# Regrouping the first two score chunks, and moving the second head pair's loads and preparation forward, in an attention and feed-forward kernel

## The chip, the cores and the metric

The kernel runs on one core of a Trainium2 chip. The metric is the device time of one execution in microseconds (us). The times of single runs are also given as the span of the trace, from first to last instruction; it is some 1.8 us shorter than the time (416.1 against 417.99 in the profiled run of the kernel before). PE does the matmuls and transposes, ACT the exponentials, DVE conversions, copies and sums; POOL issues most loads. The granted clock is the share of PE's full clock that the record of the trace gives, 1.00 or 0.50 ("half clock").

## The reference

64 heads (8 batches of 8), 1152 keys, 576 pooled queries (means of two neighbours), head size 64; then two dense layers multiplied with each other and two more layers.

```python
q_pool = q.reshape(B, H, S // 2, 2, D).mean(axis=3)
scores = (1.0 / np.sqrt(D)) * np.matmul(q_pool, k.transpose(0, 1, 3, 2))
attn = softmax(scores)
x = (attn @ v) -> (B*576, H*D)
out = ((x @ w1) * (x @ w2)) @ w3 @ w_out
```

## The kernel before

Heads go in pairs. The scores of all pairs are one long row of columns, 5184 (9 key blocks of 576 queries) for each pair, cut into 324 chunks of 512. A chunk is a few matmuls into a PSUM tile (one half for each head of the pair) and one exponential of 128 x 1024 elements on ACT. Iterations hold three chunks each; between them PE does value matmuls (`pv`), transposes of the next pair (`prep_groups`), of w3 (`w3_group`) and the feed-forward layers.

```python
js = (slice(0, 2), slice(2, 5), slice(5, NJ))   # pair 0: key blocks, three groups
...
        spin(25, 128)        # dummy matmuls, to keep PE's clock up
        stage_keys(0); move_keys(0)
        spin(8, 128)
        queries(0)           # first half of pair 0's queries: 256 of 576
        spin(6, 128)
        queries(1)           # the other 320
        spin(1)
        stage_keys(1)        # DVE: second key group to fp16
...
    def scores(c):
        t = psum.tile([128, 2, CH], FP32, tag="psc", bufs=3, name="psc")
        if 3 <= c < 10:      # filler matmul for the clock
            nc.tensor.matmul(t[:, 0], ones[:, 0:128], ones, start=True, stop=True)
        ...                  # columns c*512 to c*512+511, block by block
...
    load_v(0)                # load queue, in this order
    load_w3(0, 1)
    load_q(1)
    load_k(1)                # "pair 1's keys" below
    load_w3(1, 1)
    load_wo(0)
...
    early = [(1, w3_group(0)), (3, w3_group(1))]      # (iteration, group)
...
        if prepped < NPE:    # at the end of iteration 2: pair 1, after chunk 8
            if it >= first_it(prepped) - (1 if prepped < 5 else 2):
                queue[0:0] = prep_groups(prepped)
```

Chunks 0 to 9 belong to pair 0, and pair 1 begins inside chunk 10. PE runs in program order, so whatever stands in front of chunk 9 on PE must be done before it.

The softmax here doesn't subtract the row's maximum and nothing guards it: scores larger than these inputs give would overflow.

## Time and profile before

| | before |
|---|---|
| time, three runs | 416.72, 416.95, 418.05 us |
| span of the profiled run | 416.1 us |
| PE busy / ACT busy | 406.8 / 326.3 us |
| exponential 0 / 4 / 9 starts | 7.81 / 11.86 / 16.97 us |
| granted PE clock, 7.74 to 11.15 us | 0.50 |

The prediction shows the page and the chain of waits.

### The profile page before, as it was taken

The page shows a single profiled execution, that of the slowest core. Times are in us where ns is not written, and L with a number is a line of the kernel's source. Part 1 is how long each engine was busy: PE and PEld are TensorE (multiplying, and loading weights), DVE is VectorE, ACT ScalarE, POOL GpSimd, SP SyncE. Part 2 cuts the span into 40 slices and gives each one's busy share as a digit, 9 for nine tenths or more (in the row PEclk, how much of TensorE's full clock was granted, in tenths as well). Part 3 has the DMA queues.
Part 4 walks back from the last instruction along what each step waited for, and adds up shares of the span by engine and source line. Part 5 has one row for each costly group of instructions (what it writes and reads, how often), then busy time and mean ns, then how long its engine had stood idle before and what let it go on. Part 6 is the DMA issues. An engine that isn't in the chain of part 4 may idle for free.

```text
span 416.1 us, 12696 instructions
## 1 busy us (share of the span) xinstructions
PE 406.8 (98%) x5489; PEld 270.3 (65%) x5489; DVE 197.9 (48%) x407; ACT 326.3 (78%) x356; POOL 121.1 (29%) x161
## 2 busy tenths in 40 slices
PE   7999999999999999999999999999999999999996
PEld 5577787766676577666865686667765876544443
DVE  2455755464545553555455634544455434713141
ACT  4999989989888888988888899898888889133332
POOL 6543331243435163334433414343430000000000
PEclk8999999999999999999999999999999999999999
DMA  8999999699999999999799959999994250050402
GB/s 188 203 205 187 187 206 193 117 138 161 159 180 204 174 174 183 216 140 176 137 212 150 172 86 197 157 150 152 185 171 93 44 89 20 14 117 2 101 0 103
DMA packets 96249, 59.76 MB, mean 144 GB/s; under 512 B 65472, under 2 KB 86464, under 8 KB 96192
## 3 DMA queue, kind: packets, MB, share of 16 engines
q0 software_dynamic: 26928, 32.97, 50.8%
q1 hardware_dynamic: 69264, 25.97, 36.0%
q8 instruction: 43, 0.70, 0.7%
q14 instruction: 14, 0.11, 0.1%
HBM read 67.11 MB, written 9.44 MB: 184 GB/s over the span
## 4 chain that ended last, share of the span: by engine, by line
PE 91%; ACT 5%; DMA 1%; issue 1%; SPq 0%; DVE 0%; ACTq 0%
PE po L340 20%; PE psc L315 19%; PE pa L434 16%; PE pp L457 16%; PE pb L434 15%; ACT er L325 5%; PE pT L418 3%; DMA er<-in_k_dram 1%; PE w3t L406 1%; PE psc L305 1%; PE t L169 0%; PE tk L169 0%; SPq L192 0%; DVE kc L210 0%; SPq L189 0%
## 5 line engine op out<-in xcount | busy, mean ns | idle before, releaser
L325 ACT ACTIVATE er<-psc 128x1024 f16<-128x1024 f32 x324 | 307.5, 1027 | 41.3 <-PE psc L315 41.0
L340 PEld LDWEIGHTS <-er 128*128 128x128 f16 x2880 | 103.4, 97 | 22.0 <-issue 5.9
L340 PE MATMUL po<-vt,er 128*128 128x65 f16 x2880 | 110.4, 193 | 0.0
L315 PE MATMUL psc<-qT,kT 64*128 64x512 f16 (+7 forms) x1152 | 95.1, 286 | 3.0 <-ACT er L325 2.5
L451 DVE TENSOR_TENSOR gT<-pb,asb 128x512 f16<-128x512 f32 x72 | 50.1, 695 | 55.8 <-PE pb L434 55.1
L434 PE MATMUL pa<-xT,w1sb 128*128 128x512 f16 x288 | 74.2, 380 | 0.0
L434 PE MATMUL pb<-xT,w2sb 128*128 128x512 f16 x288 | 74.1, 380 | 0.0
L457 PE MATMUL pp<-T,gT 128*128 128x256 f16 (+1 forms) x488 | 67.9, 292 | 0.0
L315 PEld LDWEIGHTS <-kT 64*128 64x128 f16 x1152 | 45.4, 94 | 28.1 <-issue 9.5
L457 PEld LDWEIGHTS <-gT 128*128 128x128 f16 x488 | 45.6, 98 | 18.5 <-issue 3.7
L444 DVE COPY asb<-pa 128x512 f32<-128x512 f32 x56 | 38.7, 691 | 39.3 <-PE pa L434 38.1
L434 PEld LDWEIGHTS <-w2sb 128*128 128x128 f16 x288 | 26.4, 98 | 32.7 <-issue 3.9
L434 PEld LDWEIGHTS <-w1sb 128*128 128x128 f16 x288 | 25.0, 98 | 30.1 <-issue 6.2
L121 POOL TENSOR_TENSOR qp<-qst 128x1152 f16<-128x1152 f16 x12 | 28.3, 2355 | 53.5 <-issue 26.5
L469 DVE TENSOR_SCALAR osb<-pp 128x256 f32<-128x256 f32 x49 | 20.8, 424 | 39.2 <-PE pp L457 39.2
L353 DVE RECIPROCAL rz<-po 128x5 f32<-128x5 f32 x64 | 12.4, 194 | 48.5 <-PE po L340 48.1
L141 POOL COPY kc<-kst 128x576 int32<-128x576 int32 x24 | 16.4, 683 | 55.8 <-issue 43.7
L357 DVE TENSOR_TENSOR xn<-po,rz 128x320 f16<-128x320 f32 x64 | 31.5, 492 | 2.2
L95 POOL DMA_DIRECT2D vst<-in_v_dram x32 | 23.4, 741 | 11.8 <-DVE T L422 5.0
L466 ACT ACTIVATE osb<-pp 128x512 f32<-128x512 f32 (+1 forms) x12 | 7.0, 579 | 24.0 <-PE pp L457 21.8
L88 POOL DMA_DIRECT2D kst<-in_k_dram x31 | 22.6, 742 | 9.2 <-DVE kT L285 2.6
L81 POOL DMA_DIRECT2D qst<-in_q_dram x31 | 19.2, 621 | 11.4 <-DMA vst<-in_v_dram 3.5
(49 smaller groups left out, 140.6 us busy)
## 6 DMA issues: line engine op xcount, KB each, us to landing
vst<-in_v_dram POOLq DMA_DIRECT2D x32, 288.0 KB, 10.3
qst<-in_q_dram POOLq DMA_DIRECT2D x31, 288.0 KB, 7.0
kst<-in_k_dram POOLq DMA_DIRECT2D x31, 288.0 KB, 12.4
out_dram<-osb SPq DMA_DIRECT2D x66, 128.0 KB, 2.6
w3h<-in_moe_w_dram POOLq DMA_DIRECT2D x3, 512.0 KB, 14.7
xT<-in_moe_w_out_dram POOLq DMA_DIRECT2D x4, 256.0 KB, 10.7
w1sb<-in_moe_w_dram POOLq DMA_DIRECT2D x2, 512.0 KB, 16.3
w2sb<-in_moe_w_dram POOLq DMA_DIRECT2D x2, 512.0 KB, 17.0
```

What stands on the lines that cost most here:

```text
L88: nc.gpsimd.dma_start(out=kst[P].rearrange("p u j d -> p u (j d)"), in_=k[b, h0:h0 + 2].rearrange("u (p j) d -> p u (j d)", j=NJ))
L95: nc.gpsimd.dma_start(out=vst[P].rearrange("p u j d -> p u (j d)"), in_=v[b, h0:h0 + 2].rearrange("u (p j) d -> p u (j d)", j=NJ))
L121: eng.tensor_tensor(out=qps[pp][r].rearrange("p c u d -> p u c d"), in0=src[:, :, :, 0, :], in1=src[:, :, :, 1, :], op=ALU.add)
L315: nc.tensor.matmul(t[:, u, o:o + ln].rearrange("p (c f) -> p c f", f=64), kT[P][s, j, :], qT[P][s, f0 // 64:(f0 + ln) // 64], start=True, ...
L325: nc.scalar.activation(out=er[:, :, r:r + CH], in_=psc.pop(c), func=AF.Exp, bias=0.0, scale=SCALE)
L340: nc.tensor.matmul(po[P, u][:, VW * x:VW * x + D + 1], er[:, u, r:r + 128], vts[P % 4][:, u, j, 0:D + 1], start=(m == 0), stop=(m == 44), ...
L357: nc.vector.tensor_tensor(out=xn[:, P % 2, :, u, :], in0=acc[:, :, 0:D], in1=rz.to_broadcast([128, 5, D]), op=ALU.mult)
L434: nc.tensor.matmul(p, w[:, mc, ft * 128:ft * 128 + 128], xT[:, mc, t0:t0 + 512], start=(mc == 0), stop=(mc == NC - 1))
L444: nc.vector.tensor_copy(out=asb[ft], in_=p)
L451: nc.vector.tensor_mul(out=o, in0=p, in1=a)
L457: nc.tensor.matmul(p[:, 0:n], gT[:, ft, 128 * i:128 * i + 128], T16[:, ft, n * s:n * s + n], start=(ft == 0), stop=(ft == NF - 1))
L469: nc.vector.tensor_scalar_mul(out=osb, in0=p[:, 0:n], scalar1=1.0 / (SCL * SCL))
```

## The change

The intent is to start ACT earlier and to have pair 1 ready earlier. Chunk 0 is made of the first 256 queries of key blocks 0 and 1, so that it needs only the first query half; chunk 1 takes the rest of both. Pair 1's loads go ahead of w3, pair 1 is prepared ahead of chunk 8, the w3 transposes go to later iterations and one filler is deleted.

```diff
-        js = (slice(0, 2), slice(2, 5), slice(5, NJ))
+        js = (slice(0, 2), slice(2, 4), slice(4, NJ))
...
-        spin(6, 128)
+        spin(5, 128)
+        scores(0)
+        expo(0)
         queries(1)
...
-        if 3 <= c < 10:
+        if 3 <= c < 9:
...
+        if c < 2:
+            pieces = [[(0, 0, 256), (1, 0, 256)], [(0, 256, 320), (1, 256, 192)]][c]
...   (expo: chunk 0 written with a strided output, chunk 1 as two ACTIVATEs)
     load_v(0)
-    load_w3(0, 1)
     load_q(1)
     load_k(1)
+    load_w3(0, 1)
     load_w3(1, 1)
...
-    early = [(1, w3_group(0)), (3, w3_group(1))]
+    early = [(3, w3_group(0)), (4, w3_group(1))]
...
+            if it == 2 and w == 2:
+                queue[0:0] = prep_groups(1)
+                prepped = 2
+                group("F")
+                group("X")
+            if it or w:
-            scores(BURST * it + w)
-            expo(BURST * it + w)
+                scores(BURST * it + w)
+                expo(BURST * it + w)
```

More of the change, by code (lines that the diff above doesn't have):

```diff
@@ L303, in scores @@
         psc[c] = t
-        if 3 <= c < 10:
+        if 3 <= c < 9:
             nc.tensor.matmul(t[:, 0], ones[:, 0:128], ones, start=True, stop=True)
+        pieces = []
         g = c * CH
         while g < (c + 1) * CH:
-            J = g // SQ
+            J, f0 = divmod(g, SQ)
+            pieces.append((J, f0, min(SQ - f0, (c + 1) * CH - g)))
+            g += pieces[-1][2]
+        if c < 2:
+            pieces = [[(0, 0, 256), (1, 0, 256)], [(0, 256, 320), (1, 256, 192)]][c]
+        o = 0
+        for J, f0, ln in pieces:
             P, j = divmod(J, NJ)
-            f0 = g - J * SQ
-            ln = min(SQ - f0, (c + 1) * CH - g)
-            o = g - c * CH
             for u in range(2):
-                s = slice(64 * u, 64 * u + 64)
-                nc.tensor.matmul(t[:, u, o:o + ln].rearrange("p (c f) -> p c f", f=64), kT[P][s, j, :],
-                                 qT[P][s, f0 // 64:(f0 + ln) // 64], start=True, stop=True)
-            g += ln
+                x = slice(64 * u, 64 * u + 64)
+                nc.tensor.matmul(t[:, u, o:o + ln].rearrange("p (c f) -> p c f", f=64), kT[P][x, j, :],
+                                 qT[P][x, f0 // 64:(f0 + ln) // 64], start=True, stop=True)
+            o += ln
     def expo(c):
@@ L324, in expo @@
             assert nb >= 90 * Pg + 45 + 5 * Jg + 5
-        nc.scalar.activation(out=er[:, :, r:r + CH], in_=psc.pop(c), func=AF.Exp,
-                             bias=0.0, scale=SCALE)
+        t = psc.pop(c)
+        if c == 0:
+            io = [(er[:, :, 0:2 * SQ].rearrange("p u (j f) -> p u j f", j=2)[:, :, :, 0:256],
+                   t.rearrange("p u (j f) -> p u j f", j=2))]
+        elif c == 1:
+            io = [(er[:, :, 256:SQ], t[:, :, 0:320]), (er[:, :, SQ + 256:2 * CH], t[:, :, 320:CH])]
+        else:
+            io = [(er[:, :, r:r + CH], t)]
+        for o, i in io:
+            nc.scalar.activation(out=o, in_=i, func=AF.Exp, bias=0.0, scale=SCALE)
     po, xns = {}, {}
```

## The prediction

> **What bounds the kernel now.** I read the page first (shares, slices, chain), then the chain of waits for the first 45 us, then the timeline of the first 18 us, because every edit of this change lies there.
>
> ```profile
> PE 406.8 (98%) x5489; PEld 270.3 (65%) x5489; DVE 197.9 (48%) x407; ACT 326.3 (78%) x356; POOL 121.1 (29%) x161
> ...
> PE   7999999999999999999999999999999999999996
> ...
> PE 91%; ACT 5%; DMA 1%; issue 1%; SPq 0%; DVE 0%; ACTq 0%
> ```
>
> PE is busy for 406.8 of 416.1 us, and 91% of the chain that ended last is PE. So over the whole kernel PE work is the bound, and all of PE's idle time is 9.3 us. By stretches, the idle time is 2.2 us in 0 to 10, none in 10 to 15, 0.7 in 15 to 20, 1.1 in 20 to 40, 1.7 in 40 to 80, and 3.5 after 300. A reordering at the start can recover only part of the early idle time, plus whatever PE instructions it deletes.
>
> The chain of the start, in order of time (start, length, what):
>
> ```profile
> 2.23 5.12 DMA er<-in_k_dram
> 7.36 0.02 issue
> 7.38 0.76 DVE kc L210
> 8.15 0.05 issue
> 8.19 0.50 PE tk L169 x3
> 8.69 0.43 PE spin L198
> 9.12 0.54 PE psc L315 x3
> 9.66 0.54 PE psc L305
> 10.20 0.54 PE psc L315 x4
> 10.74 0.54 PE tk L169 x4
> ...
> 12.47 0.55 PE w3t L406 x8
> ...
> 16.97 1.93 ACT er L325 x2
> ```
>
> The reader should see that the first exponential is not on it. The path is the second key load of pair 0 (lands at 7.35), its conversion, its transposes, and then PE without a break from 8.19 to 16.95, up to the scores of chunk 9. ACT bounds the next stretch, from 16.97 to 23.5.
>
> The timeline shows the onset and the one gap:
>
> ```profile
> 5.94 0.37 ACT L245 CAST qT<-tq 128x256 f16<-128x256 f32 x1 [1.69 <-PE tq L242]
> 6.52 0.34 PE L240 MATMUL tq<-ident,er 64*64 64x64 f16 x10 [0.17 <-DVE er L231]
> 6.91 0.33 DVE L245 COPY qT<-tq 128x320 f16<-128x320 f16 x1 [0.44 <-PE tq L240]
> 7.81 8.93 ACT L325 ACTIVATE er<-psc 128x1024 f16<-128x1024 f32 x9 [1.49 <-PE psc L315]
> 16.97 22.32 ACT L325 ACTIVATE er<-psc 128x1024 f16<-128x1024 f32 x24 [0.24 <-PE psc L315]
> ```
>
> The first query half is in SBUF at 6.31, but exponential 0 starts at 7.81, because chunk 0 also needs the second half (ready 7.24). Nine exponentials follow, then 0.24 us of idle ACT before chunk 9. From narrow windows of the timeline they start at 7.81, 8.73, 9.70, 10.78, 11.86, 12.79, 13.88, 14.80 and 15.70. Chunks 2, 3 and 4 start 0.04 us after PE finishes their scores (9.66, 10.74, 11.82), so those three are limited by PE, not by ACT.
>
> **What the Trainium skill says.** "ScalarE: Activation LUTs", section "What ACT_TABLE_LOAD costs": an ACTIVATE with immediate scale and bias takes 186 ns + 0.833 ns per element, and back-to-back ones overlap by about 93 ns. For 1024 elements that is 1039 ns and a pitch of 946; the trace agrees, with 1027 ns and a pitch of 930 (22.32 us for 24). So splitting one exponential costs about 93 ns (an estimate from that page).
>
> "TensorE: Matmul & The Clock Gate", Part 1: a matmul starts at half clock, one per N/1.2 ns, and a free-running window of about 3.4 us of activity releases it. The trace agrees: 25 spins of 128 columns take 2.82 us, and a score chunk costs 0.54 us of chain until 10.74 and 0.32 from 11.5. The same page, Part 3, "The mechanism": matmuls start and end in program order. So a group that waits holds all PE work behind it; that is what both moved groups risk.
>
> "DMA: Bandwidth & Descriptors", "Two DMAs through the same engine are not ordered": descriptors of one queue start in order. The trace agrees in effect: loads issued in the order v0, w3 row block 0, q1, k1, w3 row block 1 release POOL's next issues at 11.21, 12.16, 13.51, 14.88 and 16.10.
>
> **Part 1, the first two chunks.** Chunk 0 becomes columns 0 to 255 of key blocks 0 and 1, which need only the first query half.
> - Release: the last such wait took 7.38 - 7.24 = 0.14 us, so its scores start at 6.31 + 0.14 = 6.45. They stream 512 columns per head as before (two pairs of 256), and exponential 0 comes 7.81 - 7.38 = 0.43 later, at 6.88: **0.93 us earlier**.
> - These scores stand ahead of the transposes of the second query half, which move from 6.52 to 6.88. Their copy ended 7.24 - 6.52 = 0.72 after they began: now 7.60, so 0.36 later.
> - Chunk 1 starts at 7.60 + 0.14 = 7.74 and is ready at 8.17. The order listing shows its second ACTIVATE with no wait, so the first waits for all four matmuls. ACT idles for some 0.3 us from 7.85 and is free again near 8.17 + 0.93 + 0.09 = 9.2.
>
> **Part 2, key groups of 2 and 5 blocks instead of 3 and 4.** Conversion of the first group starts at 7.62 (behind the later query copy), not 7.38, but is two thirds as long: 0.50, ending 8.12 against 8.13. Its transposes follow chunk 1 on PE: 8.17 + 0.33 = 8.50. The copy out takes 0.28 instead of 0.36 and ends near 8.83 against 9.09. Chunk 2 is ready at 8.86 + 0.54 = 9.40 against 9.66, chunk 3 at 10.48 against 10.74: **0.26 earlier**.
>
> Chunk 4 then pays. It needs key blocks 3 and 4. Before, block 4 was in the earlier group, and chunk 4 did not wait for the later group's copy. Now block 4 comes with the later group: five transposes, 0.54 x 5/4 = 0.67, to 11.15; copy out 0.04 + 0.42 x 5/4 = 0.57, to 11.72; a pair of 256 columns at full clock, half of 0.32, to 11.88. Exponential 4 starts at 11.92 against 11.86. **So I expect the gain of the first chunk to be spent here**, and PE to stand still for some 0.2 us that it did not stand before.
>
> **Part 3, pair 1 ahead of w3 and ahead of chunk 8.** From 11.88, PE has chunk 5 (0.64 with its filler matmul), 9 value matmuls (0.27), chunks 6 and 7 (1.28), preparation of pair 1 (0.26 + 0.61 = 0.87) and chunk 8 (0.64): 3.70, to 15.58. The w3 transposes (0.55) are gone from this stretch. Exponentials at the old pitch from 4 to 8, (15.70 - 11.86)/4 = 0.96, reach chunk 8 at 15.76: just covered. Then 13 value matmuls (0.40) and chunk 9 (0.34, its filler of about 0.3 deleted) are ready at 16.32, before ACT needs them at 16.72. The gap of 0.24 closes: exponential 9 at 16.72 against 16.97.
>
> Do the loads allow it? k1 moves from fourth to third: 11.21 + 1.35 + 1.37 = 13.93 by the spacings above. Its conversion (0.46) ends at 14.39. PE reaches the key transposes at about 14.07 + 0.35 = 14.42. Slack: almost none.
>
> **Later.** The w3 transposes (0.55 us) move to the group of iteration 3, and those of the second row block to iteration 4. Between 16.97 and 23.5 ACT bounds, and PE idles 0.52 us at 19.36, so most of the moved work fits there. Then PE is the bound and its total is smaller by one filler of 512 columns (0.3) and one short spin (0.1, but that is in time when PE waits anyway). The memory behind w3 lands in the same order; nothing later in the load queue moves. Sum: -0.25 at chunk 9, up to another -0.1 from the filler, some of it given back to moved work: **-0.3 us**.
>
> **Rivals.**
> 1. The whole 0.93 us of the first exponential survives: 416.0. For it: ACT bounds stretches up to 80 us. Against it: chunks 2 to 4 start when PE is done, so an earlier ACT only waits.
> 2. k1 lands later than 13.9, or the copies of pair 1 stall PE in front of chunk 8; 1 us late is nearly 1 us lost, 417.5 to 418. For it: slack near zero and in-order PE. Against it: it moves up by one load in a queue that keeps its order.
> 3. The clock: fewer spins and a stall let the half clock last one window more. 3.4 us at half clock is 1.7 us of PE work: 418.3. Against it: the new early scores fill what the spin leaves, and the stretch from 7.7 stays dense.
> 4. Nothing: chunk 4's wait gives all back and moved w3 work eats the gap: 416.95.
>
> **Range and chances.** 416.95 - 0.3 gives 416.6. The three runs before spread from 416.72 to 418.05, more than the effect. Rival 1 sets the low end with some spread, 415.7; rivals 2 and 4 with run noise the high end, 417.5. Two per cent is 8.3 us, more than all idle time before 300 us, so faster has 0.01; slower would need several rivals at once, 0.01.
>
> **What would show it.** First exponential at about 6.9 (step 1); a PE wait for the DVE copy of keys before chunk 4, exponential 4 within 0.2 of 11.86 (step 2); no ACT gap before chunk 9, which starts near 16.7 (step 3); total PE idle time smaller by under 0.5. I am wrong if exponential 4 is already 0.5 or more earlier, if a gap opens before chunk 8, or if the half clock lasts beyond 11.5.

## The result

| | before | after |
|---|---|---|
| median of the first comparison, 4 runs each | 417.17 us | 416.23 us |
| range | 416.72 to 418.05 | 416.03 to 416.70 |
| span of the profiled run | 416.1 us | 414.9 us |

The ratio of after to before is 0.9976, with a 95% interval of 0.9957 to 0.9996. Ratios here are the mean time of one kernel's runs over that of the other's runs of the same rounds, so not quite the ratio of the medians. 416.23 lies in the predicted range. Later calls ran the kernel before 39 more times (median 416.88, mean 416.99, from 416.13 to 419.28) and after 5 more times; all 9 runs of after have a median of 416.46 and a mean of 416.48, from 416.03 to 417.15. So the change is worth about 0.4 to 0.5 us, on a kernel whose own runs spread over 3 us. This pools several chips and has no interval of its own; by the ratios of runs of the same rounds it is 1.0 us in the first comparison and 0.3 us in the second (r_after below). The profiled run of after was the slowest of its four, that of before among the slowest of its kind.

The page of the kernel after, the lines that answer to the prediction's first fence:

```profile
PE 406.0 (98%) x5489; PEld 270.4 (65%) x5489; DVE 198.8 (48%) x407; ACT 326.3 (79%) x357; POOL 121.2 (29%) x161
...
PE   8999999999999999999999999999999999999996
...
PE 90%; ACT 6%; DMA 1%; issue 1%; SPq 0%; DVE 0%; ACTq 0%
```

Nothing changes in the large; PE's idle time is 8.9 us instead of 9.3, smaller by under 0.5 as predicted. The chain of waits of the kernel after, first 18 us:

```profile
2.23 5.47 DMA er<-in_k_dram
...
7.72 0.32 DVE kc L210
...
9.14 3.49 ACT er L340 x4
...
15.61 2.88 ACT er L340 x3
```

And ACT in its timeline (start, length, what, idle time before and who ended it):

```profile
5.21 0.37 ACT L245 CAST qT<-tq 128x256 f16<-128x256 f32 x1 [0.97 <-PE tq L242]
6.33 2.17 ACT L340 ACTIVATE er<-psc 128x1024 f16<-128x1024 f32 x3 [0.75 <-PE psc L321]
9.14 12.09 ACT L340 ACTIVATE er<-psc 128x1024 f16<-128x1024 f32 x13 [0.65 <-PE psc L321]
```

After chunk 2 the chain is ACT here, where it was PE without a break. Exponential 9 starts at 15.61 instead of 16.97, 1.36 us earlier, and the span is 1.2 us shorter. Two things differ that the change did not do directly. The first queries came earlier in this run (their copy on ACT starts at 5.21 against 5.94). And PE kept its full clock, as the busy time by stretches shows (stretch, its length, busy PE, PEld, DVE, ACT and POOL with counts, granted clock, DMA share, GB/s). Before:

```profile
8.00:9.00 1.00, 0.93 (x6) 0.35 (x4) 0.40 (x2) 1.00 (x2) 0.65 (x1) 0.50 1.09 190
```

After:

```profile
8.00:9.00 1.00, 0.90 (x7) 0.36 (x7) 0.62 (x3) 0.49 (x2) 0.61 (x1) 1.00 1.13 179
```

So two single traces cannot be set against each other as cause and effect. How much of the 1.36 us is the change, and how much is luck, is what the experiments are for.

### The profile page after: what moved, and what is told of

The parts are those of the page before. It is cut to its first block, busy times and chain, and to the rows that moved or that the text cites. A ratio compares the mean times of both kernels' runs of the same rounds, so it can differ in the third digit from the quotient of the medians.

```text
span 414.9 us, 12697 instructions
## 1 busy us (share of the span) xinstructions
PE 406.0 (98%) x5489; PEld 270.4 (65%) x5489; DVE 198.8 (48%) x407; ACT 326.3 (79%) x357; POOL 121.2 (29%) x161
## 3 DMA queue, kind: packets, MB, share of 16 engines
HBM read 67.11 MB, written 9.44 MB: 184 GB/s over the span
## 4 chain that ended last, share of the span: by engine, by line
PE 90%; ACT 6%; DMA 1%; issue 1%; SPq 0%; DVE 0%; ACTq 0%
PE po L354 20%; PE psc L321 19%; PE pa L448 16%; PE pp L471 16%; PE pb L448 15%; ACT er L340 6%; PE pT L432 3%; DMA er<-in_k_dram 1%; PE w3t L420 1%; PE t L169 0%; SPq L192 0%; SPq L189 0%; DVE osb L483 0%; DVE kc L210 0%; PE tk L169 0%
## 5 line engine op out<-in xcount | busy, mean ns | idle before, releaser
L321 PE MATMUL psc<-qT,kT 64*128 64x256 f16 (+7 forms) x1154 | 95.2, 285 | 3.0 <-ACT er L340 2.5
L456 ACT COPY asb<-pa 128x512 f32<-128x512 f32 x16 | 9.4, 585 | 16.5 <-PE pa L448 16.5
```

What stands on the lines that cost most here:

```text
L321: nc.tensor.matmul(t[:, u, o:o + ln].rearrange("p (c f) -> p c f", f=64), kT[P][x, j, :], qT[P][x, f0 // 64:(f0 + ln) // 64], start=True, ...
```

## The experiments

Twelve kernels ran, on three chips, each with 3 to 5 rounds beside the kernel before; all gave the right result. The traces give one number that ties everything together, so it comes first. "Keys" is the start of the DVE conversion of pair 1's keys, "half clock" the stretch of the first 30 us for which the trace records a granted clock of 0.50 (PE is also at half clock before that record begins, which is told under cold_before), and E9 and E20 are the starts of exponentials 9 and 20.

| kernel | half clock | keys | E9 | E20 | span | span - E9 |
|---|---|---|---|---|---|---|
| before | 7.74 to 11.15 | 14.62 | 16.97 | 27.26 | 416.1 | 399.2 |
| r_before | 15.10 to 18.51 | 14.63 | 18.01 | 28.30 | 417.5 | 399.5 |
| p1_chunks_only | 8.32 to 11.74 | 14.77 | 17.17 | 27.46 | 416.2 | 399.0 |
| p3_pair1_only | none | 12.15 | 15.46 | 26.51 | 415.4 | 399.9 |
| p3_loads | none | 12.02 | 15.31 | 25.87 | 414.7 | 399.4 |
| p3_prep | none | 13.09 | 15.90 | 26.18 | 415.0 | 399.1 |
| cold_before | none | 14.88 | 17.29 | 27.57 | 417.0 | 399.8 |
| cold_after | none | 11.99 | 15.76 | 26.32 | 415.0 | 399.3 |
| after | none | 12.05 | 15.61 | 26.17 | 414.9 | 399.3 |
| r_after | none | 12.82 | 15.51 | 26.08 | 415.0 | 399.5 |
| after_oldloads | none | 13.52 | 16.22 | 26.76 | 415.5 | 399.3 |
| after_late_pair1 | 15.80 to 22.63 | 17.43 | 21.46 | 32.01 | 420.7 | 399.3 |
| k34_after | none | 12.12 | 14.99 | 25.55 | 415.0 | 400.0 |
| after_k34_prep8 | 8.90 to 12.32 | 12.71 | 16.67 | 27.22 | 415.9 | 399.3 |

E9 moves over 6.5 us among these traces, and span minus E9 stays between 399.0 and 400.0. **A chunk 9 later than about 16 us is paid for at the end, and what happens before chunk 9 matters only if it moves chunk 9.** The 1 us of spread limits the reading: the seven traces with E9 from 14.99 to 15.90 have spans of 414.7 to 415.4 in no order, so below 16 an earlier chunk 9 is not seen to shorten the kernel.

### r_before and r_after: each kernel again

No edit. For r_before:

> The kernel before, unchanged, against itself: the noise of a comparison. Theory A (the half clock from 7.7 to 11.1 us in the profile of before is chance, a matter of where the free-running activity window falls when the kernel starts): in some runs the mean clock is 1.000 and the span is some 1 us shorter (415.1 or less), in others 0.996 and 416.1. Theory B (the half clock belongs to this kernel's idle PE before 7.7 us): every run has 0.996 and a span near 416.

For r_after:

> The kernel after, unchanged, again: 414.3 to 414.9 us of span. Theory A: among its runs some show a mean clock of 0.996 and about 1 us more. Theory B: all show 1.000, because its early scores keep PE busy enough.

r_before took 416.87 us in the median of 6 runs (416.32 to 419.28), ratio 1.0006 (0.9986 to 1.0027). r_after took 416.63 in 5 runs, ratio 0.9992 (0.9980 to 1.0004), a smaller gain than in the first comparison. The spans of before in these rounds run from 414.5 to 417.5 and those of after from 414.4 to 415.4. Theory B falls: the kernel before also reaches a mean clock of 1.000 and a span of 414.5. But theory A is too simple, because the slowest trace of before, r_before, was at full clock where the first one was at half. (It is also the slowest of all runs of before, 419.28 us, so its size is not typical.) Its chain of waits shows something else, and PE's timeline the wait:

```profile
5.23 9.38 DMA kst<-in_k_dram
...
14.63 0.47 DVE kc L165
...
15.15 1.14 PE t L169 x9
...
18.01 2.86 ACT er L325 x3
```

```profile
15.15 1.14 PE L169 MATMUL t<-ident,kc 128*128 128x128 f16 x9 [1.40 <-DVE kc L165]
```

Pair 1's keys landed only after 14.6 us. PE had done everything else and stood 1.40 us for their conversion; at 15.10, in that idle time, the clock fell to half, so the transposes of the keys took 1.14 us instead of 0.68, and chunk 9, behind them in program order, was late. In the first trace of before the same keys came at the same time (14.62), but nobody waited for them, because the half clock had made PE late anyway. The load order hides behind the clock in one run and the clock behind the load order in the other.

In r_after the second idle stretch of ACT has the same cause in small: chunk 8 stands behind pair 1's preparation, PE waits 0.45 us for the conversion of the keys (12.82), and ACT idles 0.37 us before exponential 8.

The traces also tell when the clock goes. It changes only at steps of 3.41 us. These are the windows before a step, one line for each kernel, as busy time by stretches. Before, then r_before ahead of its loss, then p1_chunks_only; all three were followed by half clock:

```profile
4.33:7.74 3.41, 2.05 (x35) 1.21 (x32) 1.60 (x4) 0.37 (x1) 3.41 (x6) 1.00 1.08 242
```

```profile
11.69:15.10 3.41, 2.07 (x22) 0.83 (x21) 1.64 (x3) 3.41 (x5) 1.00 (x3) 1.00 1.29 199
```

```profile
4.91:8.32 3.41, 2.10 (x35) 1.23 (x31) 1.47 (x3) 2.48 (x4) 3.41 (x6) 1.00 1.10 232
```

After and r_after, which kept the full clock:

```profile
6.08:9.49 3.41, 2.59 (x31) 1.10 (x27) 1.32 (x4) 2.46 (x4) 2.53 (x4) 1.00 1.07 173
```

```profile
4.29:7.70 3.41, 2.50 (x39) 1.49 (x37) 1.53 (x4) 1.49 (x3) 3.41 (x6) 1.00 1.04 238
```

Of the windows at the start that I looked at, those with 1.24 to 2.19 us of busy PE (2.19 is that of after_k34_prep8) were followed by half clock, and those with 2.50 us or more were not. That is no rule, though: near the end of the kernel such windows with 1.44 us (p1_chunks_only, 411.09 to 414.51), 1.96 (before, 410.51 to 413.93) and 2.13 (cold_before, 411.27 to 414.69) kept the full clock. PE has other work there (matmuls of up to 512 columns, no spins); no run tells what decides. At the start PE idles because data land late: in before it stood 1.00 us for the first queries. So the "luck" seems to have two parts, both different from run to run: when the first loads land, and where the 3.41 us windows lie.

### p1_chunks_only: the chunks and key groups alone

The changed kernel with the load order, the iterations of the w3 groups, the filler and the place of pair 1's preparation put back.

```diff
+    load_w3(0, 1)
     load_q(1)
     load_k(1)
-    load_w3(0, 1)
...
-        if 3 <= c < 9:
+        if 3 <= c < 10:
...
-    early = [(3, w3_group(0)), (4, w3_group(1))]
+    early = [(1, w3_group(0)), (3, w3_group(1))]
...
-            if it == 2 and w == 2:   # and its body
```

> Parts 1 and 2 alone (regrouped chunks, key groups of 2 and 5; loads, w3 groups and pair 1 as before). My prediction: exponential 0 some 0.9 us earlier but exponential 4 within 0.2 of before at equal clock, chunk 9 late again, so 0 to 0.2 us of the time. Theory B: clock 1.000 and most of the gain of the full change, 0.6 us or more.

It took 417.04 us, ratio 1.0000 (0.9986 to 1.0013): within the expectation, and theory B's 0.6 us lies just outside the interval. Its trace drew the half clock at nearly the same place as the first trace of before, which makes it the fair test of the prediction's arithmetic. ACT in its timeline:

```profile
5.97 2.17 ACT L340 ACTIVATE er<-psc 128x1024 f16<-128x1024 f32 x3 [0.48 <-PE psc L321]
9.47 2.10 ACT L340 ACTIVATE er<-psc 128x1024 f16<-128x1024 f32 x2 [1.32 <-PE psc L321]
12.06 4.87 ACT L340 ACTIVATE er<-psc 128x1024 f16<-128x1024 f32 x5 [0.49 <-PE psc L321]
17.17 22.32 ACT L340 ACTIVATE er<-psc 128x1024 f16<-128x1024 f32 x24 [0.24 <-PE psc L321]
```

Exponential 0 starts at 5.97, 1.84 us before that of before; by exponential 2 (9.47 after 1.32 us of idle time, against 9.70) only 0.23 us of it is left, by exponential 4 none. Chunk 4 is at 12.06 against 11.86, and the gap before chunk 9 is the same 0.24 us as in before. The early first chunk alone buys nothing that these runs can see.

### p3_pair1_only, p3_loads and p3_prep: the second half of the change, whole and in parts

p3_pair1_only is before with the new load order, the two later w3 groups, the early preparation (the two diffs below together) and the deleted filler:

```diff
-        if 3 <= c < 10:
+        if 3 <= c < 9:
```

p3_loads is before with the first two of these:

```diff
     load_v(0)
-    load_w3(0, 1)
     load_q(1)
     load_k(1)
+    load_w3(0, 1)
...
-    early = [(1, w3_group(0)), (3, w3_group(1))]
+    early = [(3, w3_group(0)), (4, w3_group(1))]
```

p3_prep is before with the early preparation alone:

```diff
+            if it == 2 and w == 2:
+                queue[0:0] = prep_groups(1)
+                prepped = 2
+                group("F")
+                group("X")
             scores(BURST * it + w)
```

> Part 3 alone (pair 1 loaded ahead of w3 and prepared ahead of chunk 8, filler of chunk 9 deleted, w3 groups later; first chunks as before). My prediction: the gap before chunk 9 closes and PE has less to do there, 0.2 to 0.4 us faster. Theory B: clock 0.996 as before, and little of the gain.

> Before, with only the load order and the two later w3 groups of part 3 (pair 1 is prepared after chunk 8 as before, filler of chunk 9 kept). Theory C (the time is set by the start of chunk 9: the span ends some 399.3 us after it, and what the change does is to move pair 1's keys forward so that PE never waits for them): no PE wait for the DVE conversion of pair 1's keys, exponential 9 near 15.6 to 16.2 in a run at full clock, span = that + 399 to 400, mean time as the full change within 0.3 us. My prediction's rival (the order of loads hardly matters; the chunk regrouping or the early preparation carries the gain): exponential 9 not before 16.7.

> Before, with only the preparation of pair 1 moved ahead of chunk 8 (loads in the old order). Theory C: pair 1's keys land fourth, near 14.6, so PE stands before chunk 8 for 0.5 to 1.5 us, ACT has a gap there, exponential 9 at 17 or later and the mean time 0.3 to 1 us above before. Rival: the preparation's place is what closes the gap, and this is as fast as part 3.

| | median | ratio to before (95%) |
|---|---|---|
| p3_pair1_only | 417.14 us | 1.0005 (0.9993 to 1.0017) |
| p3_loads | 416.69 us | 0.9999 (0.9981 to 1.0017) |
| p3_prep | 416.67 us | 0.9993 (0.9977 to 1.0009) |

By the times, none of the three can be told from before. That is a miss for the prediction, which gave p3_pair1_only, all of part 3, a gain of 0.2 to 0.4 us (by its interval a gain of more than 0.3 us is excluded), and a miss for theory C as a statement on mean times of parts. By the traces, p3_loads behaves as theory C said: no PE wait for the keys' conversion (12.02), ACT without a gap before chunk 9, E9 at 15.31. p3_prep was expected to be slower, and was not: its keys, still fourth in the queue, came at 13.09 in that trace, not at 14.6, and PE waited only 0.27 us. How late a load lands varies by about as much as its place in the queue gains: where DVE waited for the fourth load, it began at 13.09 (p3_prep), 13.52 (after_oldloads) and 14.63 (r_before), where it waited for the third, from 12.02 to 12.82.

p3_pair1_only shows why an early chunk 9 is not always kept. Its E9 is 15.46, but E20 follows 11.05 us later instead of 10.29: DVE waits for the queries of pair 2. Its timeline of DVE:

```profile
21.44 0.75 DVE L121 TENSOR_TENSOR qp<-qst 64x1152 f16<-64x1152 f16 x1 [0.62 <-DMA qst<-in_q_dram]
```

The chain of r_after also passes through that load (it ends at 20.98). So the next load can be the next bound: landing at 20.98 it delayed nothing in r_after (E20 10.57 after E9), landing at 21.41 it did.

E20 minus E9 gives one more clean number. It is 10.28 or 10.29 us in the five traces with the w3 groups in iterations 1 and 3, and 10.54 to 10.57 in the eight others with them in 3 and 4 (p3_pair1_only aside). The work moved out of the way of chunk 9 costs 0.27 us later. How much of that reaches the end is not shown: span minus E9 is 399.3 in the mean of the five and 399.4 in that of the eight. In the chain of after it can be seen where, ahead of chunk 15:

```profile
19.18 0.45 PE w3t L420 x8
19.63 0.87 PE pT L432 x8
...
21.39 1.03 ACT er L340
```

In before, ACT itself was the chain there, from 20.60 to 23.50. Now the extra transposes of w3 (the first line) make PE the chain, and ACT idles 0.16 us before 21.39.

### cold_before and cold_after: without the short spins

Both kernels without their short spins (in after the third is `spin(5, 128)`):

```diff
-        spin(25, 128)
...
-        spin(8, 128)
...
-        spin(6, 128)
```

> Before without its 39 short spins of 128 columns, so that PE is idle for most of the first 5 us and the half clock should be drawn in most runs. Theory A (the clock is a draw, and at half clock PE bounds the stretch to chunk 9): mean clock 0.99 or below, exponential 9 at 17 or later, span 416.5 or more. If the clock does not matter: spans as before, 414.5 to 416.

> After without its 38 short spins. If the gain is that the change keeps the clock up, it falls to the time of cold_before. Theory C: it keeps an advantage of 0.3 to 1 us over cold_before, because PE has less to do before chunk 9 (w3 group and one filler fewer, some 0.9 us at full clock, more at half).

cold_before took 417.45 us, ratio 1.0020 (1.0001 to 1.0040), and cold_after 417.37, ratio 1.0018 (0.9996 to 1.0040). So in before the spins are worth some 0.8 us (0.2% of 417, with an interval that almost reaches zero), and without them the change shows no advantage in the times: cold_after spreads from 416.80 to 419.11. The expected 0.3 to 1 us is not there. The two traces, at E9 17.29 and 15.76, differ in when the full clock came, 11.91 us in one and 9.46 in the other; PE in cold_before was busy throughout between these times, so an estimate of that part is half of the 2.45 us, 1.2 of the 1.53 us.

The mean clock was 1.000 in cold_before, against the expectation, and the reason is worth knowing: the record of the clock begins with its first change. Cold_before, busy time by stretches and PE's timeline:

```profile
10.00:11.00 1.00, 1.00 (x9) 0.48 (x9) 0.00 (x0) 0.94 (x2) 0.49 (x1) 1.00 1.13 200
```

```profile
9.57 0.61 PE L302 MATMUL psc<-const-bfloat16-1.0 128*128 128x512 bf16 x1
...
12.06 0.39 PE L302 MATMUL psc<-const-bfloat16-1.0 128*128 128x512 bf16 x1
```

The column says 1.00, and the same filler takes 0.61 us at 9.57 and 0.39 at 12.06. PE was at half clock, and the column did not know it yet.

### after_late_pair1 and after_oldloads: how far does a late load reach?

after_late_pair1 puts pair 1's loads behind both w3 row blocks and half of w_out; after_oldloads puts only w3 row block 0 back in front of them.

```diff
     load_v(0)
-    load_q(1)
-    load_k(1)
     load_w3(0, 1)
     load_w3(1, 1)
     load_wo(0)
+    load_q(1)
+    load_k(1)
```

```diff
     load_v(0)
+    load_w3(0, 1)
     load_q(1)
     load_k(1)
-    load_w3(0, 1)
     load_w3(1, 1)
```

> After, with pair 1's query and key loads issued behind both w3 row blocks and the first half of w_out (sixth and seventh in the queue instead of second and third). Theory C in numbers: keys land some 4 to 5 us later than the 12.0 to 12.8 of after (estimate from 1.2 to 1.4 us per load in the traces), conversion starts near 17, PE stands before chunk 8 for some 3 to 5 us, exponential 9 starts some 2.8 us after the conversion, near 19.5 to 20, and the span is that + 399.0 to 399.9, so 418.5 to 420. If the start of chunk 9 did not set the end, ACT or PE would catch up later and the span would stay under 417.

> After, with only the load order undone (w3 row block 0 ahead of pair 1; its group still in iteration 3). Theory C: keys land between 13.0 and 14.6, PE waits for their conversion 0.5 to 2 us ahead of chunk 8, exponential 9 at 15.9 to 17.5, span that + 399.3; in the mean of all runs some 0.5 us above after. If p3_prep's 15.9 was typical: hardly slower than after.

after_late_pair1 took 422.48 us, ratio 1.0143 (1.0116 to 1.0169), the one clear effect. The chain of waits of its trace:

```profile
7.29 10.11 DMA kst<-in_k_dram
...
17.43 0.47 DVE kc L165
...
21.46 2.86 ACT er L340 x3
```

The landing (17.4) was as expected; chunk 9 came 4.0 us after it instead of 2.8, because PE stood 3.22 us for the queries alone and worked at half clock for 6.83 us. From chunk 9 to the end it was 399.3 us, as in the other traces. Nothing catches up. This settles theory C's main sentence for a delay of this size: against after, chunk 9 came 5.85 us later and the span is 5.8 us longer.

after_oldloads took 417.27 us, ratio 1.0008 (0.9986 to 1.0030), with single runs from 416.32 to 418.19. Its trace had the keys at 13.52, a PE wait of 0.55, an ACT gap of 0.47 before chunk 8 and E9 at 16.22, all inside the expectation. Its mean time is 0.8 us above that of all 9 runs of after (417.24 against 416.48), where 0.5 was expected.

### k34_after and after_k34_prep8: the key groups, and a version meant to beat both

```diff
-        js = (slice(0, 2), slice(2, 4), slice(4, NJ))
+        js = (slice(0, 2), slice(2, 5), slice(5, NJ))
```

after_k34_prep8 has this edit and takes out the early preparation:

```diff
-            if it == 2 and w == 2:
-                queue[0:0] = prep_groups(1)
-                prepped = 2
-                group("F")
-                group("X")
```

> After, with the old key groups of 3 and 4 blocks instead of 2 and 5. My prediction's step 2: block 4 is back in the earlier group, the wait of PE for the DVE copy ahead of chunk 4 (0.15 us in both traces of after) is gone and exponential 4 follows 3 at the usual pitch of 0.91 us instead of 0.97; chunk 2 is some 0.1 us later. Together no more than 0.1 us of the time. Rival: the groups of 2 and 5 matter for the whole, 0.3 us or more slower.

> A version meant to beat both: after with the old key groups of 3 and 4 blocks and with pair 1 prepared after chunk 8, as before (load order, later w3 groups, early chunk 0 and deleted filler stay). No wait for pair 1's keys can then hold chunk 8; exponential 9 at 15.0 to 15.3 where the second key load lands by 7.1, span 414.3 to 414.7, at best 0.3 us under after, within the noise of a single run.

The wait that the first asks about, in PE's timeline of the kernel after:

```profile
10.72 0.28 PE L321 MATMUL psc<-qT,kT 64*128 64x256 f16 x2 [0.15 <-DVE kT L226]
```

In k34_after it is gone, and exponential 4 follows 3 by 0.90 us instead of 0.98. So the groups of 2 and 5 cost ACT 0.08 us, no more. k34_after took 416.33 us (416.21 to 416.73, 6 runs), ratio 0.9986 (0.9965 to 1.0007): the lowest median of all experiments (only p3_prep has a narrower range), with E9 at 14.99, but not separated from before or from after by its interval.

after_k34_prep8 took 416.84, ratio 1.0004 (0.9983 to 1.0025). Its trace drew the half clock from 8.90 to 12.32 and has E9 at 16.67. The expected 0.3 us under after and chunk 9 at 15.0 to 15.3 did not come.

## Why the prediction was right or wrong

**The time: right.** Predicted 416.6, range 415.7 to 417.5; measured 416.23 in the first comparison and 416.46 over all 9 runs. The predicted gain was 0.3 us; measured were 1.0 and 0.3 us in the two comparisons, 0.4 to 0.5 us over all runs. That proves little about the mechanism: the range also holds most runs of before, and the sum came out near the mark with terms wrong in opposite directions. Of the three signs that the prediction named for being wrong, two came: exponential 4 was 0.8 us earlier (after), and a gap opened before chunk 8 (0.37 us in r_after).

**What bounds the kernel: half right.** That the part of the early idle time that can be won lies before chunk 9 fits the 14 traces. But the prediction took the half clock of the one trace as a property of the kernel. It was a draw: the same kernel also runs that stretch at full clock, and then, in the one such trace, pair 1's keys bound it (r_before).

**Step 1, the first chunk: right.** Predicted from the end of the query copy to exponential 0: 6.88 - 6.31 = 0.57 us. Measured: 6.33 - 5.58 = 0.75 in after, 6.51 - 6.03 = 0.48 in r_after, 0.48 in p1_chunks_only; before had 1.50. (That it starts at 6.33 and 6.51 instead of 6.88 is due to earlier queries.) The split of exponential 1 was put at 0.09 us; in r_after its two parts take 0.97 us from start to next start where one takes 0.91, so 0.06.

**Step 2, chunks 2 to 4: right at half clock, wrong at full clock.** Predicted exponentials 2, 3 and 4 at 9.44, 10.52 and 11.92; p1_chunks_only has 9.47, 10.55 and 12.06. At full clock (after) they are at 9.14, 10.06 and 11.04, so the stated sign of error, exponential 4 "already 0.5 or more earlier", came true. "I expect the gain of the first chunk to be spent here" failed there: the wait for the later key group is real (0.15 us of PE) but costs 0.06 to 0.08 us of ACT. The gain is spent elsewhere: before chunk 2 in after, where ACT idles 0.65 us because the second key load of pair 0 landed only at 7.70; before chunk 8 in r_after.

**Step 3, pair 1: right in direction, mis-sized.** Predicted exponential 9 at 16.72, 0.25 us earlier; the traces of after have 15.61 and 15.51. Much of that is the draw: the mean spans (414.71 in 9 runs of after, 415.21 in 39 of before) are only 0.50 us apart. The term counted only the visible gap of 0.24 us at half clock. At full clock the wait for pair 1's keys can go as well (1.40 us in r_before, none in after), and the trace that the prediction was made from could not show it. As the source of the gain this step is not shown: alone (p3_pair1_only) it gave none in the times.

**The landing of pair 1's keys:** predicted 13.93 with almost no slack. The conversion started at 12.05 and 12.82. The spacings were as predicted (in after POOL's issues are released at 9.52, 10.89 and 12.31), but the first load of the queue was done by 9.52, not 11.21. In the first trace the slack was 0.9 us (conversion done at 12.51, PE there at 13.41); in the second PE waited 0.45. Rival 2 is therefore real in some runs, at a third of its stated size.

**Later: wrong in sign.** The prediction gave up to another 0.1 us of gain. The w3 group moved to iteration 4 costs 0.27 us between chunks 9 and 20, in the eight traces that can be compared.

**Rivals 1, 3 and 4.** The whole gain of the first exponential does not survive (p1_chunks_only: no gain). The clock rival was seen in single runs of both kinds of kernel, though in neither trace of after. "Nothing" is not excluded by the second comparison alone (interval up to 1.0004), but is by the first (up to 0.9996).

**What stays open.** No part of the change alone is faster than before outside the noise, so how the 0.5 us divide between load order, early preparation and early chunk is not settled. The later w3 groups, which take 0.55 us of transposes away from before chunk 9, were never moved alone. k34_after, with a mean of 416.38 us, can be set beside two kernels of the same rounds that undo one part more, after_k34_prep8 without the early preparation (417.06) and after_oldloads with the old load order (417.24; it also has the groups of 2 and 5). Both are 0.7 to 0.9 us slower and have runs at 417.7 and above, where k34_after stays under 416.8. With the rest in place both moves may thus be needed; six runs each, and no interval. The fastest runs of before (414.4 us of span) and after (414.3) are equal. 12 of the 39 runs of before took longer than 417.2 us and none of the 9 of after. That fits a change which takes away bad draws more than it lowers the best time; with 9 runs this is a reading, not a proof.

## What to carry to other kernels

Find the instruction after which every trace takes the same time to the end (here exponential 9, 399 to 400 us), and judge any change of the start by when that instruction begins; but look also for the point from which an earlier start no longer shows in the span (here about 16 us). Before a prediction, look at the granted clock of each stretch and at when the first loads land, and ask what would bind if that one run's clock or landing had been different: a wait can hide behind a slow clock. Loading late what the whole engine order stands behind cost 5.8 us here; moving it forward by one place, alone, gave nothing that the times show. An early start of the consumer bought nothing before the second load was there.

## What the Trainium skill lacked or had wrong

- "TensorE: Matmul & The Clock Gate", Part 1, names an idle window as what takes the clock back to half. Here the half clock also followed windows with PE busy for 2.05 to 2.19 of their 3.41 us, while others with 1.44 to 2.13 us kept the full clock; the page does not say what decides. The length of the window, 3.41 us, agrees.
- The same page, on records of the clock: in these traces the record begins with its first change (4.3 to 11.9 us in), and until then the granted clock reads 1.00 while a matmul of 512 columns takes 0.61 us instead of 0.39. Its general warning about such records applies; this form of it is not there.
- "ScalarE: Activation LUTs", "What ACT_TABLE_LOAD costs": the split of one exponential costs 93 ns by its overlap rule (an estimate from the page); about 60 ns were measured. One of 1024 elements agrees (1027 ns against 1039), but back to back they start 0.90 to 0.92 us apart, not 0.946; the prediction's 930 ns is 22.32 us divided by 24, small waits included.
- "DMA: Bandwidth & Descriptors" has nothing on how far the landing of one load varies from run to run with 16 busy engines: where DVE waited for it, the conversion of what the fourth load brings began between 13.09 and 14.63 us (three traces), and of what the third brings between 12.02 and 12.82 (five).
